# The second tile's edge masks made by two predicated copies on VectorE, and dense work divided among the attention blocks by another rule

## The chip, the core and the metric

The kernel runs on one core of a Trainium2 chip. A core has a matrix engine (TensorE, PE in the profile), a vector engine (VectorE, DVE), an engine for activation functions (ScalarE, ACT), GpSimd (POOL), and SyncE (SP), whose queue issues most of the DMAs here. The engines run side by side, each its own list of instructions in order, and wait for one another by semaphores. Data lies in HBM, in SBUF (128 partitions) and in PSUM (128 partitions, where TensorE writes its results).

The metric is the time of one execution on the device in microseconds (us); the median of several runs counts. The profiler traces one execution with the start and the length of its instructions, and its page and views sum these up.

## The reference

Four residual layers act on x (2048 rows, 640 columns), attention and feed-forward in turn, twice, all with the same weights.

```python
def _A_ref(x, wqkv, wo):
    H = 32; Dh = D // H; W = 256
    q, k, v = ...                        # (x @ wqkv), 32 heads of 20
    scores = jnp.einsum("bhqd,bhkd->bhqk", q, k) * (Dh ** -0.5)
    mask = (idx[:, None] - idx[None, :] >= 0) & (idx[:, None] - idx[None, :] < W)
    scores = jnp.where(mask[None, None], scores, -1e9)
    p = _softmax(scores, axis=-1)
    o = jnp.einsum("bhqk,bhkd->bhqd", p, v)
    return o.transpose(...).reshape(B, S, D) @ wo
def _B_ref(x, w1, b1, w2, b2):
    h = jnp.einsum("bsd,df->bsf", x, w1) + b1
    h = relu(h) ** 2
    return jnp.einsum("bsf,fd->bsd", h, w2) + b2
x = x + _A_ref(_layernorm(x), ...); x = x + _B_ref(_layernorm(x), ...)   # twice
```

A query sees the 256 keys up to and with its own. So of a block of scores of 64 keys by 64 queries, those on the two edges of this band are cut by a diagonal: on the near edge the keys behind the query's own position fall out, on the far edge those 256 or more before it.

## The kernel before

**Units and quads.** The 2048 rows are worked in units of T = 256 rows, 8 for each of the two pairs of layers, 16 in all (u = 0 to 15). A unit has dense work (projections to q, k and v, the projection after attention, the feed-forward layer) and attention work. Dense matmuls fill the whole 128x128 array; each product is a sum of three f16 matmuls (`mm3`, line 327). Attention works on quads of four heads, 8 quads a unit, n = 0 to 127. For units that have a unit of their own sequence before them (14 of 16, so 112 quads) the blocks are cut into tiles of 64 rows and a quad has three blocks on TensorE:

- M (`max_quad`, line 661): q times k with keys along the columns, only for each row's largest score. It works for a quad some places ahead (LEAD = 3). VectorE then moves the far-edge scores that count over others with a predicated copy (line 674, mask `maskq`) and reduces (line 677), for each of the two tiles e = 0 and 1.
- S (`exp_quad` and `halves_quad`, line 796): k times q with keys along the partitions, with the largest score subtracted by two more rows of the product. ScalarE takes the exponentials (line 781), two of 128x640 for each tile, into the SBUF tile `pt`. Then the band's edges are set to zero in `pt` by GpSimd's selects (line 809): for each tile, each of two edges (k) and each half of the partitions (h), one select on 64x256 elements, eight a quad. `masks[0]` holds the four jobs that the first two steps of V need, `masks[1]` those of the last two.
- V (`pv_quad`, line 874): probabilities times values, summed over four steps k; before step k it waits for `masks[k // 2]`. One part of its result goes to a bank that dense accumulators use too, and ScalarE copies it out (line 885); another goes to a spare part of M's and S's banks, and VectorE adds it (line 888, the job in `pvfree`).

S, M and V write the same six banks or wait for one another: S and M wait for the jobs in `bbjobs`, that is, M for the exponentials and S for the reductions.

Units 0 and 8 have whole tiles (lines 692, 830, 840); the change doesn't touch these but in a modelled time.

**The planner.** Each engine's order is written out when the program is built, by a model of time. `now` is TensorE's modelled clock. `post(eng, cost, fn, *deps, prio=...)` makes a job for an engine with a modelled cost; `pump` places jobs that can start, those of lower `prio` first, which `urgency` names by kind. `step(ns)` lets the clock go on by a dense piece of about 500 ns, and `Stream` hands out such pieces.

`together` (line 1162) lays the quads of one unit over dense work. `turns` gives two entries a quad, for S and for V; when an M is due it stands directly in front of V. Each entry has a part of the dense work, SHARE of a quad's between S and V and the rest between V and the next S. `work(part, w)` places dense pieces until that part is done and the jobs of the block are ready by the model. In front of V it is called again, with `pvfree`, the jobs of `masks[0]`, and those of `masks[1]` less 600 ns; where these aren't ready, dense pieces go between M and V.

`CARRY`, `KEEP` and `MID` are amounts of dense work kept for the last unit, for what follows its last quad, and for a place within it.

Of the kernel before, what the change touches and what calls it, by code (L numbers as in the profile page):

```python
# [16 lines left out]
P = 128  # L17
# [28 lines left out]
def kernel(ctx: ExitStack, tc: tile.TileContext, x, wqkv, wo, w1, b1, w2, b2, out):  # L46
# [11 lines left out]
    nc.vector.memset(neghalf, -0.5)  # L58
    masks = sb.tile([P, 3 * P], BF16, name="pt", tag="pt", bufs=2)
    maskq = sb.tile([P, Q], BF16, name="maskq")  # L60
    maskw = sb.tile([P, 2 * P], BF16, name="maskw")
# [9 lines left out]
    for h in range(2):  # L71
        nc.gpsimd.tensor_copy(maskq[h * Q:(h + 1) * Q, :], masks[h * Q:(h + 1) * Q, (h + 4) * Q:(h + 5) * Q])
    b1s = sb.tile([P, FC], F32, name="b1s")
    kts = []
# [30 lines left out]
    LOOK, LAT, LAND, CROSS, WLAND = 250.0, 50.0, 1800.0, 3600.0, 4500.0  # L105
    rate = [335.0]
    TAIL = {"A": 115.0, "D": 85.0, "G": 40.0, "S": 0.0}
# [66 lines left out]
    def step(ns):  # L174
        now[0] += ns
        pump()
# [142 lines left out]

    urgency = {"out": 0, "od": 0.5, "cross": 1, "mask": 0.5, "turn": 0.5, "exp": 0.5, "ln": 1, "y": 0.5}  # L320

# [303 lines left out]
    def max_quad(n, later=False):  # L625
# [19 lines left out]
        if quarters(u):  # L645
# [20 lines left out]
            by_tiles(pieces)  # L666
            now[0] += 763.0
            for e in range(2):
# [18 lines left out]
        else:  # L687
            for w in range(4):
                j, i = divmod(w, 2)
                for e in range(2):  # L690
                    r, p = slice(64 * e, 64 * e + 3 * DH), 2 * qd + j
                    nc.tensor.matmul(bb[e][:, w % 3, w // 3 * T:w // 3 * T + (1 + i) * P], qt[r, p, i * P:(i + 1) * P],  # L692
                                     cur[r, p, :(1 + i) * P], start=True, stop=True)
            now[0] += 440.0
            for w in range(4):
# [87 lines left out]
    def halves_quad(n, u, qd, qt, flat):  # L783

        pieces = []
        for j in range(2):
            for h in range(2):
                for kb, (o, q0, w) in PARTS[h].items():
                    kt, k0 = kts[(u if kb >= 2 else u - 1) % 3], kb % 2 * P + h * Q
                    a, b = (10 * j + o) * Q, (10 * j + o + w) * Q  # L790
                    cuts = [a] + [z for z in (512, 1024) if a < z < b] + [b]
                    for c0, c1 in zip(cuts, cuts[1:]):

                        def put(e, kt=kt, k0=k0, j=j, q=q0 * Q + c0 - a, c0=c0, c1=c1, h=h):
                            r = slice(64 * e, 64 * e + 3 * DH + 2)
                            nc.tensor.matmul(flat[e][h * Q:(h + 1) * Q, c0:c1], kt[r, 2 * qd + j, k0:k0 + Q],  # L796
                                             qt[r, 2 * qd + j, q:q + c1 - c0], start=True, stop=True,
                                             tile_position=(64 * e, 64 * h))

                        pieces.append((h, c1 - c0, put))  # L800
        by_tiles(pieces)
        now[0] += 763.0
        boxes, masks = [{}, {}], [[], []]
        for e, box in enumerate(boxes):

            def mask(k, h, box=box):
                r = slice(h * Q, (h + 1) * Q)
                m = box["pt"].rearrange("p (g c) -> p g c", g=4)[r, :, 4 * Q * k:4 * Q * k + Q]
                nc.gpsimd.affine_select(out=m, in_=m, pattern=[[0, 4], [-1 if k else 1, Q]], base=0, fill=0.0,  # L809
                                        compare_op=ALU.is_gt if k else ALU.is_ge, channel_multiplier=1 if k else -1)  # L810

            exps = []
            for j in range(2):
                exps.append(post("A", 584, power(box, flat[e], 10 * Q * j, 10 * Q * (j + 1)), *exps, prio=urgency["exp"]))
            bbjobs.extend(exps)
            for at, (k, h) in enumerate(((0, 0), (1, 1), (1, 0), (0, 1))):
                masks[at // 2].append(post("G", 415, lambda k=k, h=h, mask=mask: mask(k, h), *exps,
                                           prio=0 if n > NQ * NU - 4 else urgency["mask"]))
        return boxes, masks

    def whole_quad(n, u, qd, qt, flat):
# [3 lines left out]
        for k in range(2):  # L825
            w = T - k * P
            for j in range(2):
                for e in range(2):
                    r = slice(64 * e, 64 * e + 3 * DH + 2)
                    nc.tensor.matmul(flat[e][:, 512 * k + w * j:512 * k + w * (j + 1)], cur[r, 2 * qd + j, k * P:(k + 1) * P],  # L830
                                     qt[r, 2 * qd + j, k * P:T], start=True, stop=True)
        now[0] += 530.0
        for k in range(2):
# [16 lines left out]
    def pv_quad(n, quad):  # L850
# [8 lines left out]
        for k in range(4 if halves else 2):  # L859
            need(*masks[k // 2 if halves else k])  # L860
            for j in range(2):
                for e in range(2):
                    jj = 2 * j + e
                    c = (4 * qd + jj) * (DH + 1)
                    for h in range(2 if halves else 1):
# [5 lines left out]
                        else:  # L871
# [4 lines left out]
                                         skip_group_check=True, tile_position=(h * Q, 32 * jj))  # L876
            now[0] += (450.0, 230.0, 330.0, 285.0)[k] if halves else 400.0
        if qd == 0:
# [244 lines left out]

    SHARE = 0.5
    ALONE = 0.7
# [36 lines left out]
    def together(ns, ms, dense, cost, share=1.0, whole=True, after=None, pace=0):  # L1162
# [6 lines left out]

        def work(part, w):  # L1170

            nonlocal done
            while True:
                t = when(w) if w else None
                ready = t is not None and t <= now[0]
                if done >= cost * share * part / total and (ready or not w):
                    return
                c = s.go()
# [7 lines left out]
        for k, (part_, what, m) in enumerate(ts):  # L1186
# [6 lines left out]
            if kind == "s":  # L1193
                wants += pvfree
            work(part, Want(*wants, bank=False))
            if kind == "s":
# [27 lines left out]

    QKC, VC, OC, FCST, LNC, CARRY, KEEP, MID = 16.4e3, 8.2e3, 8.2e3, 39.2e3, 1.2e3, 22e3, 28e3, 10e3

# [77 lines left out]
    for u in range(1, NU):  # L1304
        last = u == NU - 1
        if u == 2:
            urgency.update({"out": 0, "od": 1, "cross": 0.5, "mask": 0, "turn": 0.5, "exp": 0.5, "ln": 0.5, "y": 1})
        quads, ahead = range(NQ * u, NQ * (u + 1)), range(NQ * u + LEAD, NQ * (u + 1) + LEAD)
# [46 lines left out]
```

## Time and profile before

| what | value |
|---|---|
| median of three runs | 1592.25 us (1591.53 to 1593.83) |
| the profiled execution, and its span | 1591.27 us, 1589.5 us |
| mean granted TensorE clock of the profiled execution | 0.997 of full speed |
| exponentials, line 781 | 512, 684 ns in the mean |
| selects, line 809 | 896, 440 ns in the mean, 394.0 us in all |
| predicated copies of line 674 | 224, 425 ns in the mean |
| reductions, line 677 | 224, 1222 ns in the mean |
| selects: shortest, median, longest | 406, 413, 1022 ns |

How to read the views. The page gives busy times by engine, the chain of work that ended last, and groups of instructions (line, engine, operation, output<-inputs, shapes, count; busy us, mean ns of one; the engine's idle time before them and what ended most of it). PE are matmuls, PEld the loads of their stationary operand. A row of the timeline has the start from the span's beginning, the length from the first instruction's start to the last one's end (us), engine, line, operation and a count where several were merged, and in brackets an idle time before it with what ended it. Matmuls overlap in their pipeline: what one costs is seen from start to start, not from its length. Where V's rows are shown, the first of its 64 stands for the block. A row of a line's own view, such as "POOL pt L809: 16.4, 64", names who ended the engine's idle time before that line's instructions, the sum in us, and how many times.

### The profile page before, as it was taken

How to read it: one execution, taken by the hardware profiler on the slowest of the kernel's cores; microseconds unless marked ns; L12 is line 12 of the kernel's file. 1: busy time of each engine (PE TensorE's matmuls, PEld its weight loads, DVE VectorE, ACT ScalarE, POOL GpSimd, SP SyncE). 2: the span in 40 equal slices, each digit the busy share in tenths (PEclk: the TensorE clock that was granted, in tenths of full speed). 3: DMA queues.
4: the chain of work that ended last, by engine and by line, in shares of the span. 5: the costliest groups of instructions: out<-in, count | busy, mean ns of one | idle time of the engine just before them, and what ended most of it. 6: DMA issues, size and time to landing. Idle time of an engine off the chain costs nothing.

```text
span 1589.5 us, 59412 instructions
## 1 busy us (share of the span) xinstructions
PE 1558.7 (98%) x25842; PEld 1200.2 (76%) x25842; DVE 971.3 (61%) x2022; ACT 669.1 (42%) x1369; POOL 636.2 (40%) x1291
## 2 busy tenths in 40 slices
PE   8989999999999999999999999999999999999989
PEld 7667777777777877778777777877778777786767
DVE  8787675655756466565565756566665656656432
ACT  4554435344343433434344343434434344443512
POOL 1224435344352533535233353533535344354612
PEclk9999999999999999999999999999999999999999
DMA  9874254442434334343352535425343351431020
GB/s 272 205 207 101 53 120 90 119 96 72 117 76 127 85 96 111 67 119 80 109 125 74 119 74 125 99 82 121 60 121 92 103 115 51 115 79 58 30 66 18
DMA packets 243375, 160.90 MB, mean 101 GB/s; under 512 B 91177, under 2 KB 226857, under 8 KB 243113
## 3 DMA queue, kind: packets, MB, share of 16 engines
q1 hardware_dynamic: 236744, 147.58, 38.2%
q10 hardware_dynamic: 6368, 9.50, 2.0%
q8 instruction: 203, 3.33, 0.9%
q14 instruction: 60, 0.48, 0.1%
HBM read 84.68 MB, written 52.95 MB: 87 GB/s over the span
## 4 chain that ended last, share of the span: by engine, by line
PE 92%; DVE 3%; DMA 1%; ACT 1%; issue 1%; POOL 1%; SPq 0%; POOLq 0%; ACTq 0%; DVEq 0%
PE acc L327 70%; PE pv L874 8%; PE bb L796 5%; PE bb L661 5%; PE bb L874 3%; DVE bb L641 1%; DVE mx L677 0%; ACT pt L781 0%; DMA kt<-in_B_w_dram 0%; PE spin L341 0%; PE bb L830 0%; PE bb L692 0%; POOL pt L809 0%; DMA o<-ot 0%; DMA qt<-mT 0%
## 5 line engine op out<-in xcount | busy, mean ns | idle before, releaser
L809 POOL TENSOR_SCALAR_AFFINE_SELECT pt<-pt 64x256 f32<-64x256 f32 x896 | 394.0, 440 | 523.4 <-ACT pt L781 458.0
L781 ACT ACTIVATE pt<-bb 128x640 f32<-128x640 f32 (+2 forms) x512 | 309.6, 684 | 245.9 <-PE bb L796 214.0
L327 PE MATMUL acc<-y,w_s 128*128 128x256 f16 x2880 | 336.3, 274 | 1.2 <-ACT y L377 0.6
L327 PE MATMUL acc<-w_s,hh 128*128 128x320 f16 (+1 forms) x2340 | 329.3, 297 | 0.0
L327 PEld LDWEIGHTS <-w_s 128*128 128x128 f16 x2880 | 275.8, 98 | 44.0 <-issue 2.4
L327 PEld LDWEIGHTS <-hh 128*128 128x128 f16 x2340 | 220.5, 98 | 87.2 <-issue 0.6
L677 DVE TENSOR_REDUCE mx<-bb 128x4 f32<-128x1024 f32 x224 | 273.8, 1222 | 6.3
L327 PE MATMUL acc<-yT,wq_s 128*128 128x256 f16 x2250 | 259.5, 273 | 2.2 <-DVE qd L510 0.7
L327 PEld LDWEIGHTS <-wq_s 128*128 128x128 f16 x2400 | 229.2, 98 | 37.4 <-issue 3.5
L674 DVE COPY_PREDICATED bb<-maskq,bb 128x256 f32<-128x256 uint16 x224 | 95.2, 425 | 156.0 <-PE bb L661 138.0
L1065 POOL TENSOR_TENSOR r<-r 128x256 f32<-128x256 f32 x192 | 120.3, 647 | 162.8 <-ACT r L1061 159.9
L1071 DVE TENSOR_TENSOR hh<-r,hh 128x256 f16<-128x256 f32 x192 | 94.7, 527 | 144.4 <-ACT hh L1068 135.9
L874 PE MATMUL pv<-pt,vt 64*32 64x128 f32 (+5 forms) x3840 | 180.7, 303 | 0.8 <-issue 0.6
L885 ACT COPY ot<-pv 128x256 f32<-128x256 f32 x128 | 47.5, 371 | 281.0 <-PE bb L874 260.8
L874 PE MATMUL bb<-pt,vt 64*32 64x192 f32 (+3 forms) x3584 | 164.2, 301 | 0.6 <-POOL pt L809 0.3
L874 PEld LDWEIGHTS pv<-pt,vt 64*32 64x32 f32 (+1 forms) x3840 | 128.4, 106 | 38.0 <-POOL pt L809 9.0
L327 PE MATMUL acc<-wo_s,od 128*128 128x320 f16 x960 | 142.8, 302 | 5.3 <-ACT od L965 2.8
L327 PE MATMUL acc<-wq_s,yT 128*128 128x320 f16 x900 | 132.8, 299 | 1.1 <-DVE y L378 0.5
L327 PEld LDWEIGHTS <-od 128*128 128x128 f16 x960 | 91.4, 98 | 46.9 <-ACT od L965 3.5
L874 PEld LDWEIGHTS bb<-pt,vt 64*32 64x32 f32 x3584 | 118.1, 105 | 10.7 <-POOL pt L809 7.1
L1061 ACT ACTIVATE r<-acc,b1s 128x256 f32<-128x256 f32 x192 | 80.7, 471 | 100.6 <-PE acc L327 98.3
L1068 ACT CAST hh<-r 128x256 f16<-128x256 f32 x192 | 74.5, 408 | 91.2 <-POOL r L1065 90.4
(99 smaller groups left out, 1376.1 us busy)
## 6 DMA issues: line engine op xcount, KB each, us to landing
qt<-qk SPq DMA_DIRECT2D x30, 480.0 KB
kt<-qk SPq DMA_DIRECT2D x30, 480.0 KB
qk<-qd SPq DMA_DIRECT2D x17, 640.0 KB
o<-ot SPq DMA_DIRECT2D x256, 42.0 KB
od<-o SPq DMA_DIRECT2D x14, 640.0 KB
qk<-yl SPq DMA_DIRECT2D x13, 640.0 KB
qk<-qd SPq DMA_DIRECT2D x17, 320.0 KB
xt<-in_A_x_dram SPq DMA_DIRECT2D x16, 320.0 KB
```

The source lines that it names most:

```text
L327: nc.tensor.matmul(acc, lhs(a, c), rhs(b, c), start=(k == 0), stop=(k == 3 * nk - 1))
L661: nc.tensor.matmul(flat[e][rows, o:o + b - a], qt[r, p, i * P + 64 * h:i * P + 64 * (h + 1)], kt[r, p, a + to:b + to], start=True, stop=Tr ...
L674: nc.vector.copy_predicated(wins[:, :, 4 * Q:], later, wins[:, :, :Q])
L677: nc.vector.tensor_reduce(most, wins[:, :, Q:], axis=mybir.AxisListType.X, op=ALU.max)
L781: return lambda: nc.scalar.activation(room_of(box)[:, a:b], bank[:, a:b], AF.Exp, scale=SCALE / (QS * QS))
L796: nc.tensor.matmul(flat[e][h * Q:(h + 1) * Q, c0:c1], kt[r, 2 * qd + j, k0:k0 + Q], qt[r, 2 * qd + j, q:q + c1 - c0], start=True, stop=Tru ...
L809: nc.gpsimd.affine_select(out=m, in_=m, pattern=[[0, 4], [-1 if k else 1, Q]], base=0, fill=0.0, compare_op=ALU.is_gt if k else ALU.is_ge, ...
L874: nc.tensor.matmul(pv[h][32 * jj:32 * (jj + 1), q0 * Q:(q0 + w) * Q], vf[r, c:c + 32], boxes[e]["pt"][r, a:b], start=(k == 0), stop=(k == ...
L1061: nc.scalar.activation(box["r"], acc[:, f, :], AF.Relu, bias=b1s[:, f0 + f:f0 + f + 1], scale=1.0 / (YS * WS))
L1065: nc.gpsimd.tensor_tensor(box["r"], box["r"], box["r"], op=ALU.mult)
L1068: nc.scalar.copy(hh[:, 0, f, :], box["r"])
L1071: nc.vector.tensor_sub(hh[:, 1, f, :], box["r"], hh[:, 0, f, :])
```

## The change

For the second tile (e = 1) of each of the 112 quads with half tiles, the four selects on GpSimd are replaced by two predicated copies on VectorE, one for each edge k, over all 128 partitions and 256 elements, that write zeros where a mask `drop` says so. Both stand in `masks[0]` and `masks[1]`. The first tile keeps its four selects. `drop` is made once at the start.

The planner is changed too: the modelled costs of S, M and V; 110 ns that the next dense piece is charged after each of these blocks; the order of urgencies, and from which unit on the second set of them holds; SHARE 0.6 instead of 0.5; CARRY 18 and MID 8 us instead of 22 and 10. In front of an M that is followed by V, `work` takes a further condition `hope`: beyond its part it goes on with dense pieces until `pvfree` and the masks are at most 600 ns (`masks[0]`) and 1200 ns (`masks[1]`) away, or 3 us of dense work have been done above the part.

```diff
+    edges = sb.tile([P, 2, P], BF16, name="pt", tag="pt", bufs=2)
+    drop = sb.tile([P, 2, Q], BF16, name="drop")
+    zero = sb.tile([P, 1], F32, name="zero")
+    nc.vector.memset(zero, 0.0)
+    nc.vector.memset(edges, 1.0)
...
+    nc.gpsimd.affine_select(out=edges[:, 0], in_=edges[:, 0], pattern=[[-1, P]], compare_op=ALU.is_gt,
+                            fill=0.0, base=0, channel_multiplier=1)
+    nc.gpsimd.affine_select(out=edges[:, 1], in_=edges[:, 1], pattern=[[1, P]], compare_op=ALU.is_ge,
+                            fill=0.0, base=0, channel_multiplier=-1)
+    for h in range(2):
+        nc.gpsimd.tensor_copy(drop[h * Q:(h + 1) * Q], edges[h * Q:(h + 1) * Q, :, h * Q:(h + 1) * Q])
...
-    rate = [335.0]
+    rate, apart, SWITCH = [335.0], [False], 110.0
...
     def step(ns):
-        now[0] += ns
+        now[0] += ns + (SWITCH if apart[0] else 0.0)
+        apart[0] = False
         pump()
...
-    urgency = {"out": 0, "od": 0.5, "cross": 1, "mask": 0.5, "turn": 0.5, "exp": 0.5, "ln": 1, "y": 0.5}
+    urgency = {"out": 0, "od": 0.5, "cross": 2, "mask": 0, "turn": 1, "exp": 0.5, "ln": 1, "y": 1, "clear": 0.5}
...
-            now[0] += 763.0
+            now[0] += 690.0
+            apart[0] = True
...
+            def clear(k, box=box):
+                m = box["pt"].rearrange("p (g c) -> p g c", g=4)[:, :, 4 * Q * k:4 * Q * k + Q]
+                nc.vector.copy_predicated(m, drop[:, k:k + 1, :].bitcast(mybir.dt.uint16).to_broadcast([P, 4, Q]),
+                                          zero.unsqueeze(1).to_broadcast([P, 4, Q]))
+
+            if e:
+                for k in range(2):
+                    j = post("D", 340, lambda k=k, clear=clear: clear(k), *exps, prio=urgency["clear"])
+                    masks[0].append(j)
+                    masks[1].append(j)
+                continue
...
-            now[0] += (450.0, 230.0, 330.0, 285.0)[k] if halves else 400.0
+            now[0] += (440.0, 225.0, 330.0, 305.0)[k] if halves else 420.0
+        apart[0] = True
...
-    SHARE = 0.5
+    SHARE = 0.6
+    HOPE = 3000.0
...
-                if done >= cost * share * part / total and (ready or not w):
-                    return
+                ahead = done - cost * share * part / total
+                if ahead >= 0 and (ready or not w):
+                    t = when(hope) if hope and ahead < HOPE else 0.0
+                    if t is not None and t <= now[0]:
+                        return
...
-            work(part, Want(*wants, bank=False))
+            hope = None
+            if kind == "v" and m is not None:
+                hope = Want(*pvfree, bank=False, soon=[(j, 600.0) for j in quad[1][0]] + [(j, 1200.0) for j in quad[1][-1]])
+            work(part, Want(*wants, bank=False), hope)
...
-    QKC, VC, OC, FCST, LNC, CARRY, KEEP, MID = 16.4e3, 8.2e3, 8.2e3, 39.2e3, 1.2e3, 22e3, 28e3, 10e3
+    QKC, VC, OC, FCST, LNC, CARRY, KEEP, MID = 16.4e3, 8.2e3, 8.2e3, 39.2e3, 1.2e3, 18e3, 28e3, 8e3
...
-        if u == 2:
-            urgency.update({"out": 0, "od": 1, "cross": 0.5, "mask": 0, "turn": 0.5, "exp": 0.5, "ln": 0.5, "y": 1})
+        if u == 1:
+            urgency.update({"out": 0, "od": 1, "cross": 0.5, "mask": 0, "turn": 0.7, "exp": 0.5, "ln": 0.5, "y": 0.5, "clear": 0})
```

More of the change, by code (lines that the diff above doesn't have):

```diff
@@ L693, in max_quad @@
                                      cur[r, p, :(1 + i) * P], start=True, stop=True)
-            now[0] += 440.0
+            now[0] += 530.0
+            apart[0] = True
             for w in range(4):
@@ L801, in halves_quad @@
         by_tiles(pieces)
-        now[0] += 763.0
+        now[0] += 690.0
+        apart[0] = True
         boxes, masks = [{}, {}], [[], []]
@@ L831, in whole_quad @@
                                      qt[r, 2 * qd + j, k * P:T], start=True, stop=True)
-        now[0] += 530.0
+        now[0] += 540.0
+        apart[0] = True
         for k in range(2):
@@ L876, in pv_quad @@
                                          skip_group_check=True, tile_position=(h * Q, 32 * jj))
-            now[0] += (450.0, 230.0, 330.0, 285.0)[k] if halves else 400.0
+            now[0] += (440.0, 225.0, 330.0, 305.0)[k] if halves else 420.0
+        apart[0] = True
         if qd == 0:
@@ L1168, in together, with work @@
         s = Stream(dense)
-        def work(part, w):
+        def work(part, w, hope=None):
             nonlocal done
```

## The prediction

> **What bounds the kernel now.** I read the page's first and fourth parts, the waits, a table by windows, and then the timeline around single quads. The page first: span, busy time by engine, and the chain that ended last.
>
> ```profile
> span 1589.5 us, 59412 instructions
> PE 1558.7 (98%) x25842; PEld 1200.2 (76%) x25842; DVE 971.3 (61%) x2022; ACT 669.1 (42%) x1369; POOL 636.2 (40%) x1291
> PE 92%; DVE 3%; DMA 1%; ACT 1%; issue 1%; POOL 1%; SPq 0%; POOLq 0%; ACTq 0%; DVEq 0%
> ```
>
> TensorE is busy 98% of the span and makes 92% of the chain; no other engine is near full. So time can only come off in two ways: TensorE waits less, or its own instructions take less. The change alters no matmul. The profiled execution took 1591.27 us, 1.77 us more than its span and 0.98 us under the median of 1592.25 us; a saving worked out on it is taken off the median unchanged.
>
> The next fence has one unit of the steady middle by windows (columns: window, length, busy us of PE, PEld, DVE, ACT, POOL), and from the view of line 874, whose matmuls multiply probabilities and values, the row that says for what TensorE stood idle in front of it.
>
> ```profile
> 850.00:946.30 96.30, 96.29 (x1601) 74.44 (x1600) 59.03 (x111) 39.90 (x82) 38.15 (x79) 1.00 0.40 98
> ...
>   POOL pt L809: 16.4, 64
> ```
>
> A unit of eight quads takes 96.30 us, 12.04 us a quad. TensorE waited 64 times, 16.4 us in all, for the masks that GpSimd makes with the selects of line 809. That is the largest wait the change can touch.
>
> Now the order inside a quad, by starts on TensorE. L796 is the score block (S), L661 the block for the maxima of a later quad (M), L874 the values block (V, first row shown), L327 dense work.
>
> ```profile
> 869.93 5.09 PE L327 MATMUL acc<-yT,wq_s 128*128 128x256 f16 x45
> 874.95 0.76 PE L661 MATMUL bb<-kt,qt 60*64 60x256 f16 x38
> 875.64 0.40 PE L874 MATMUL pv<-pt,vt 64*32 64x256 f32 x1
> 876.94 1.27 PE L327 MATMUL acc<-yT,wq_s 128*128 128x256 f16 x10
> ...
> 1309.80 0.76 PE L661 MATMUL bb<-kt,qt 60*64 60x256 f16 x38
> 1310.49 0.72 PE L327 MATMUL acc<-y,w_s 128*128 128x256 f16 x5
> 1311.14 0.40 PE L874 MATMUL pv<-pt,vt 64*32 64x256 f32 x1
> 1312.44 4.12 PE L327 MATMUL acc<-y,w_s 128*128 128x256 f16 x35
> ```
>
> Start to next start: 45 dense matmuls take 5.02 us, 5 take 0.65. So one costs (5.02 - 0.65) / 40 = 0.109 us, and each run of dense work costs 0.65 - 5 x 0.109 = **0.10 us on top**, whatever its length. M takes 0.69 whether V or dense follows, V takes 1.30 whether M or dense stood before it. So a short dense run between M and V costs 0.10 us more than the same matmuls put into the next run. Such runs stand between M and V in 47 of the 112 quads with half-tile masks; of the short ones (up to ten matmuls) these are the first and the last.
>
> ```profile
> 291.03 0.72 PE L327 MATMUL acc<-w_s,hh 128*128 128x320 f16 x4
> ...
> 1485.22 0.72 PE L327 MATMUL acc<-y,w_s 128*128 128x256 f16 x5
> ```
>
> **The change part by part.**
>
> *The masks.* One quad with its neighbours on all engines:
>
> ```profile
> 886.82 0.76 PE L661 MATMUL bb<-kt,qt 60*64 60x256 f16 x38
> 887.62 0.43 DVE L674 COPY_PREDICATED bb<-maskq,bb 128x256 f32<-128x256 uint16 x1
> 888.09 1.22 DVE L677 TENSOR_REDUCE mx<-bb 128x4 f32<-128x1024 f32 x1
> 888.88 4.83 PE L327 MATMUL acc<-wo_s,od 128*128 128x320 f16 x33
> 889.90 0.42 DVE L674 COPY_PREDICATED bb<-maskq,bb 128x256 f32<-128x256 uint16 x1
> 890.43 0.42 DVE L888 TENSOR_TENSOR ot<-bb,ot 128x256 f32<-128x256 f32 x1
> 890.77 1.21 DVE L677 TENSOR_REDUCE mx<-bb 128x4 f32<-128x1024 f32 x1
> 893.64 0.76 PE L796 MATMUL bb<-qt,kt 62*64 62x128 f16 x38
> 894.58 2.49 ACT L781 ACTIVATE pt<-bb 128x640 f32<-128x640 f32 x4 [5.16 <-PE bb L796]
> 895.95 4.30 POOL L809 TENSOR_SCALAR_AFFINE_SELECT pt<-pt 64x256 f32<-64x256 f32 x8 [1.65 <-ACT pt L781]
> 898.65 0.76 PE L661 MATMUL bb<-kt,qt 60*64 60x256 f16 x38
> 899.34 0.40 PE L874 MATMUL pv<-pt,vt 64*32 64x256 f32 x1
> 900.89 2.36 PE L327 MATMUL acc<-yT,wq_s 128*128 128x256 f16 x20
> ```
>
> From S's start the four exponentials end at +3.43 us, the eight selects at +6.61. V starts at +5.70 and takes 1.55 instead of 1.30: its last part waits for the last selects. After the change GpSimd has four selects, 4 x 0.54 (4.30 / 8) from +2.31, done at +4.5; VectorE starts two copies behind the last exponential. The trace has no predicated copy on this tile. Nearest row: line 674 with the same 128x256 elements, 0.43; its operands lie elsewhere (scores in PSUM). Bounds for one copy: 0.42, a lone 128x256 operation on SBUF, and 0.56, the same one beside GpSimd, both shown below under the rivals; I take 0.43. Two end at +4.4 (+4.7 at the upper bound, if VectorE is free). So the masks are ready about 2 us sooner.
>
> *Where V will stand.* The share of dense work between S and V rises from 0.5 to 0.6. Dense time of a quad: 12.04 - 0.69 (S) - 0.69 (M) - 1.30 (V) - 0.21 (two runs) = 9.15 us. V comes at 0.69 + 0.10 + 0.6 x 9.15 + 0.69 = +6.97 us, 2.3 us after the later mask. The 16.4 us can go between not at all and wholly; I take **11 us**, two thirds, since the waits in the first unit, in the last two (less dense work a quad) and in three quads without an M have less cover. Once they go, V follows M at once; what is late next is the bank into which the next dense run writes, and that wait stays.
>
> *Fewer runs.* Dense work now goes on in front of M until the masks are nearly there, by up to 3 us more than the share asks, instead of splitting in two around M. Bounds: none of the 47 runs goes, or all, 4.9 us. I take 42, **4.4 us**, for with masks at +4.7 M and V fit together in nearly every quad. The Trainium skill (TensorEngine Tiling, Key Properties) says that a change of tiling mode drains TensorE, not only a change between dense and tiled; M and V here use different tile shapes, so by it M next to V would still pay one of the two drains and the saving be 2.2 us, the sum 1583. The trace disagrees: M is 0.69 and V 1.30 with or without dense work between.
>
> *VectorE's bill.* 224 copies x 0.43 = 96 us more, 971 to 1067 us, 67% of the span. In the chain VectorE holds 3%, 48 us, of which I let a tenth more come back in proportion to the tenth more work: **4 us** lost (bounds: nothing, and 0.10 us a quad or more, the fourth rival). Queued behind a copy that waits for its exponential stand evictions of dense accumulators, the reductions of line 677 and the sum of line 888; the next dense run waits for the first, S for the others. The cover is that exponentials end 3.5 us before V, and S, M and V stand apart.
>
> *GpSimd's relief.* 448 selects x 0.44 go, 197 us. GpSimd is off the path but for V's wait, so this is worth nothing beyond the masks.
>
> *The rest.* The planner's constants (cost of S, M, V, 110 ns for a switch, urgencies, 4 us of dense work moved out of the last unit) change order only: 0, with 2 us either way. Setup adds two selects, two small copies and two memsets. Nearest rows:
>
> ```profile
> L63 DVE MEMSET maskw<- 128x128 uint32 x1 | 0.2, 165 | 0.0
> masks.py:199 POOL TENSOR_SCALAR_AFFINE_SELECT ident<-ident 128x128 f32<-128x128 f32 x1 | 0.3, 294 | 0.1
> L72 POOL COPY maskq<-pt 64x64 bf16<-64x64 bf16 x2 | 0.5, 232 | 0.1
> ```
>
> Some 0.2 us on VectorE and 2 x 0.294 + 2 x 0.232 = 1.05 us on GpSimd, once, at the start; I count nothing for it. No DMA is added or moved past a queue.
>
> **Sum:** -11 - 4.4 + 4 = -11.4 us. 1591.27 becomes 1579.9; on the median's scale 1592.25 - 11.4 = **1581 us**.
>
> **The rivals.**
>
> *1. Copies and selects hold each other up.* Line 1071's subtraction has two inputs in SBUF, as the new copy has (mask and zero):
>
> ```profile
> 1133.73 1.47 POOL L1065 TENSOR_TENSOR r<-r 128x256 f32<-128x256 f32 x2 [1.54 <-ACT r L1061]
> 1134.92 0.56 DVE L1071 TENSOR_TENSOR hh<-r,hh 128x256 f16<-128x256 f32 x1 [0.19 <-ACT hh L1068]
> 1135.67 0.43 DVE L1071 TENSOR_TENSOR hh<-r,hh 128x256 f16<-128x256 f32 x1 [0.19 <-ACT hh L1068]
> ...
> L1071 DVE TENSOR_TENSOR hh<-r,hh 128x256 f16<-128x256 f32 x192 | 94.7, 527 | 144.4 <-ACT hh L1068 135.9
> ```
>
> With GpSimd at work it took 0.56 us, with GpSimd idle 0.43; the mean of all is 527 ns. The second tile's copies run just when the first tile's selects run. The cost would be 224 x 0.13 = 29 us of VectorE; V has 2.3 us of cover, so it decides only where that is used up. If half of the wait for masks stays (5.5) and VectorE's bill grows by 1.4: 1588 us. The Trainium skill (SBUF — State Buffer, Who interferes with whom) states such a lock for VectorE with two SBUF inputs against a GpSimd operation that reads SBUF; these rows agree.
>
> *2. The order doesn't change.* If the new condition in front of M seldom binds, the short runs stay: 1581 + 4.4 = 1585 us. For it: 65 of 112 quads already go without. Against: the masks come 2 us sooner.
>
> *3. The wait moves from selects to copies.* If VectorE reaches the copies late, V waits as long for them: only 4.4 - 4 is left, 1592 us, no change. It needs copies that start 2.5 us after the last exponential, two reductions of 1.22 us in front. At 61% busy that is rare.
>
> *4. Slower: S waits for the reductions.* With 0.4 x 9.15 = 3.66 us of dense work between V and S instead of 4.76 (888.88 to 893.64), S comes 1.0 us earlier after V. The second reduction ended at 891.98, 1.66 us before S; 0.66 us is left. If displaced evictions make it 1.0 us late, S waits 0.34 us; in half of the quads, 56 x 0.34 = 19 us: 1600 us. It decides from 11.4 / 112 = 0.10 us a quad, a reduction 0.76 us late. Against it: the planner lays dense work in front of S when it sees the reduction late, so only what it misjudges (2 x 0.13 us of copies) counts.
>
> **How the numbers follow.** Forecast 0.55; first rival 0.12 (1588); second 0.13 (1585); third 0.10 (1592); fourth 0.10 (1600). About 0.2%, 3.2 us, is what a measurement here can tell from no change, so faster means under 1589.1. The forecast, the second and most of the first lie there: **0.79**; the third and the first's rest within: **0.11**; slower **0.10**. The low end is all of 16.4 and 4.9 with nothing lost, 1571; the high end reaches the third rival, 1592; the fourth and the far tails are left out.
>
> **What would show it.** Right: the wait of line 874 for GpSimd's masks falls from 16.4 to a few us; under ten dense runs between M and V; a unit of about 95.6 us instead of 96.30; VectorE near 1067 us, GpSimd near 440. Wrong: line 874 waiting for the new copies (third), the copies well over 0.5 us with waits for masks left (first), the short runs still there (second), or TensorE idle in front of line 796 for VectorE (fourth).

## The result and the profile after

| | median us | lowest to highest | executions |
|---|---|---|---|
| before | 1591.89 | 1591.45 to 1593.83 | 4 |
| after | 1573.45 | 1572.40 to 1574.43 | 4 |

The ratio is 0.9882 (95% interval 0.9865 to 0.9899): 18.4 us less, where 11.4 were forecast. The profiled execution took 1573.51 us, 17.8 less than that of before, with a span of 1571.8. From the page of the changed kernel: span, busy time by engine, the chain by engine, and of the groups the first tile's selects and the new copies.

```profile
span 1571.8 us, 58938 instructions
...
PE 1541.4 (98%) x25842; PEld 1202.1 (76%) x25842; DVE 1041.4 (66%) x2248; ACT 669.1 (43%) x1369; POOL 453.6 (29%) x847
...
PE 79%; DVE 7%; POOL 2%; issue 2%; ACT 1%; DMA 0%; SPq 0%; ACTq 0%; DVEq 0%; POOLq 0%
...
L824 POOL TENSOR_SCALAR_AFFINE_SELECT pt<-pt 64x256 f32<-64x256 f32 x448 | 195.4, 436 | 619.2 <-ACT pt L795 589.7
...
L833 DVE COPY_PREDICATED_SCALAR pt<-drop,zero 128x256 f32 x224 | 99.7, 498 | 178.9 <-ACT pt L795 178.2
```

In the changed file the score block S is line 810, M 673, V 901, dense work 339, the selects 824, the copies 833, the reductions 690, the exponentials 795. The view of V's line says for what TensorE stood idle in front of it.

```profile
its engine sat idle before it (us, times) until:
  issue: 3.7, 18
  POOL pt L867: 2.2, 8
  POOL r L1093: 0.2, 1
  DVE bmv L369: 0.2, 1
  DVE pt L833: 0.2, 1
```

The selects, 16.4 us and 64 times before, are gone from the list (line 867 belongs to the units with whole tiles); the copies took their place once, for 0.2 us. One quad by the timeline of the changed kernel, with one row for V:

```profile
869.49 0.76 PE L810 MATMUL bb<-qt,kt 62*64 62x128 f16 x38
870.18 5.63 PE L339 MATMUL acc<-yT,wq_s 128*128 128x256 f16 x50
870.34 2.49 ACT L795 ACTIVATE pt<-bb 128x640 f32<-128x640 f32 x4 [3.69 <-PE bb L810]
871.76 1.84 POOL L824 TENSOR_SCALAR_AFFINE_SELECT pt<-pt 64x256 f32<-64x256 f32 x4 [9.73 <-ACT pt L795]
872.94 0.89 DVE L833 COPY_PREDICATED_SCALAR pt<-drop,zero 128x256 f32 x2 [2.86 <-ACT pt L795]
...
875.74 0.76 PE L673 MATMUL bb<-kt,qt 60*64 60x256 f16 x38
876.43 0.40 PE L901 MATMUL pv<-pt,vt 64*32 64x256 f32 x1
...
877.73 2.90 PE L339 MATMUL acc<-yT,wq_s 128*128 128x256 f16 x25
```

From S's start the last exponential ends at +3.34 us, the selects at +4.11, the copies at +4.34. V starts at +6.94 and takes 1.30 (876.43 to 877.73), with nothing between M and V. That is the forecast order and nearly its times: copies at +4.4, V at +6.97; the selects, forecast at +4.5, are done 0.4 sooner.

**Where the 17.7 us of span came from.** I divided both traces at the first V row of the 17th quad (unit 2) and of the 113th (unit 14): a start, a middle of twelve units, and the end with what follows the last quad. By windows (length, busy us of PE, PEld, DVE, ACT, POOL, then TensorE's granted clock), the kernel before:

```profile
0.00:206.40 206.40, 191.56 (x2715) 144.26 (x2715) 153.58 (x390) 103.29 (x206) 68.36 (x141) 0.99 0.63 168
206.40:1358.30 1151.90, 1148.60 (x19703) 889.96 (x19699) 701.58 (x1410) 481.99 (x984) 479.13 (x976) 1.00 0.41 98
1358.30:1586.40 228.10, 218.51 (x3429) 165.96 (x3428) 115.85 (x222) 83.78 (x179) 88.75 (x175) 0.99 0.22 58
```

and the changed kernel, with one unit of its middle:

```profile
0.00:215.40 215.40, 195.47 (x2725) 146.79 (x2726) 161.24 (x410) 103.21 (x206) 51.55 (x109) 0.96 0.58 160
215.40:1352.80 1137.40, 1134.45 (x19700) 890.20 (x19696) 754.96 (x1584) 480.28 (x984) 338.75 (x624) 1.00 0.41 99
1352.80:1568.80 216.00, 211.45 (x3432) 165.09 (x3428) 124.89 (x253) 85.60 (x179) 63.31 (x114) 0.99 0.22 61
...
850.00:945.30 95.30, 95.23 (x1599) 74.33 (x1597) 63.09 (x125) 39.74 (x82) 28.91 (x53) 1.00 0.40 99
```

The stretches hold the same matmuls, to within ten. The start is 9.0 us longer, the middle 14.5 shorter (1.2 a unit), the end 12.1 shorter. Only the middle was in my sum. To see what they are made of, I took each block's time on TensorE from its start to the next block's start, less its bare cost from the prediction (S and M 0.69, V 1.30, a dense run 0.10 and 0.109 a matmul of 256 columns, others in proportion to their columns); S, M and V here are those of the 112 quads with half tiles. In the middle V's excess falls from 9.4 us to 0.2, the dense runs from 226 to 192 (34 x 0.10 = 3.4) and their excess from 3.9 to 0.9; S's excess rises from 4.0 to 5.2. With five dense matmuls fewer (0.5) and the blocks with whole tiles 0.6 longer that makes the 14.5. The end's 12.1 are V (3.0), S (2.6), the excess of dense runs (3.3), seven runs fewer (0.7) and the transposes of line 391 (3.4), with M 0.9 longer. Over the whole execution V's excess goes from 18.4 to 5.3, dense runs from 312 to 266, and runs between M and V from 47 to 2.

Of the 5.3, 4.2 stand at one place, behind the first V of unit 1. It is the dense run after this V that waits there, not V for a mask, and the kernel before has 3.7 us at the same place:

```profile
126.36 7.04 PE L339 MATMUL acc<-wo_s,od 128*128 128x320 f16 x30 [3.81 <-ACT od L993]
```

### The profile page after: what moved, and what is told of

Read it like the earlier page. It is cut to its first block, busy times and chain, and to the rows that moved or that the text cites. A ratio compares the mean times of both kernels' runs of the same rounds, so it can differ in the third digit from the quotient of the medians.

```text
span 1571.8 us, 58938 instructions
## 1 busy us (share of the span) xinstructions
PE 1541.4 (98%) x25842; PEld 1202.1 (76%) x25842; DVE 1041.4 (66%) x2248; ACT 669.1 (43%) x1369; POOL 453.6 (29%) x847
## 4 chain that ended last, share of the span: by engine, by line
PE 79%; DVE 7%; POOL 2%; issue 2%; ACT 1%; DMA 0%; SPq 0%; ACTq 0%; DVEq 0%; POOLq 0%
PE acc L339 61%; PE pv L901 6%; PE bb L810 5%; PE bb L673 4%; DVE mx L690 2%; PE bb L901 2%; POOL bmv L376 1%; POOL pt L824 1%; ACT pt L795 1%; DVE xt L378 1%; DVE bb L687 1%; DVE x L1128 0%; DVE bst L365 0%; DVE ot L916 0%; DVE bb L653 0%
## 5 line engine op out<-in xcount | busy, mean ns | idle before, releaser
L824 POOL TENSOR_SCALAR_AFFINE_SELECT pt<-pt 64x256 f32<-64x256 f32 x448 | 195.4, 436 | 619.2 <-ACT pt L795 589.7
L339 PE MATMUL acc<-y,w_s 128*128 128x256 f16 x2880 | 328.9, 273 | 1.3 <-DVE y L390 1.2
L833 DVE COPY_PREDICATED_SCALAR pt<-drop,zero 128x256 f32 x224 | 99.7, 498 | 178.9 <-ACT pt L795 178.2
L901 PE MATMUL pv<-pt,vt 64*32 64x192 f32 (+5 forms) x3840 | 167.8, 304 | 0.5 <-POOL pt L867 0.3
L901 PE MATMUL bb<-pt,vt 64*32 64x64 f32 (+3 forms) x3584 | 153.9, 301 | 0.0
```

The lines of the kernel that those rows point to most:

```text
L339: nc.tensor.matmul(acc, lhs(a, c), rhs(b, c), start=(k == 0), stop=(k == 3 * nk - 1))
L833: nc.vector.copy_predicated(m, drop[:, k:k + 1, :].bitcast(mybir.dt.uint16).to_broadcast([P, 4, Q]), zero.unsqueeze(1).to_broadcast([P, 4, ...
L901: nc.tensor.matmul(pv[h][32 * jj:32 * (jj + 1), q0 * Q:(q0 + w) * Q], vf[r, c:c + 32], boxes[e]["pt"][r, a:b], start=(k == 0), stop=(k == ...
```

## The experiments

Theory A: the gain is the sooner masks, and the planner's constants fit the new timing. Rival B: it is the planner's order, which the masks merely permit. Rival C: the copies cost VectorE much more than is seen, and something else pays for it. The same three stretches tell the runs apart; the stretches are bounded as above in each trace, and "runs" are dense runs in the middle.

| kernel | median us (before beside it) | ratio, 95% | start | middle | end | runs |
|---|---|---|---|---|---|---|
| before, profile above | 1591.89 | | 206.4 | 1151.9 | 228.1 | 226 |
| before, once more | 1591.27 (one execution) | | 207.5 | 1152.3 | 226.6 | 226 |
| after, profile above | 1573.45 (1591.89) | 0.9882, 0.9865 to 0.9899 | 215.4 | 1137.4 | 216.0 | 192 |
| after, once more | 1575.51 (1591.70) | 0.9900, 0.9886 to 0.9914 | 218.7 | 1137.3 | 216.8 | 192 |
| masks only | 1576.74 (1592.27) | 0.9901, 0.9886 to 0.9917 | 215.8 | 1142.2 | 225.7 | 193 |
| masks only, once more | 1580.11 (1591.70; one execution) | | 209.0 | 1140.0 | 226.3 | 193 |
| planner only | 1621.44 (1592.27) | 1.0189, 1.0168 to 1.0210 | 220.5 | 1163.3 | 234.0 | 192 |
| no `hope` | 1587.12 (1592.27) | 0.9964, 0.9950 to 0.9978 | 215.2 | 1138.8 | 231.5 | 192 |
| copies twice | 1602.93 (1592.27) | 1.0069, 1.0050 to 1.0088 | 216.4 | 1154.1 | 224.3 | 192 |
| unit 1 with selects | 1578.19 (1589.85) | 0.9918, 0.9902 to 0.9933 | 219.9 | 1139.0 | 216.0 | 192 |
| CARRY 22, MID 10 | 1582.46 (1589.85) | 0.9955, 0.9942 to 0.9967 | 216.9 | 1137.5 | 223.3 | 193 |
| zero as a whole tile | 1581.91 (1589.85) | 0.9949, 0.9934 to 0.9963 | 217.5 | 1141.9 | 218.2 | 192 |
| SHARE 0.5 | 1588.44 (1589.85) | 0.9989, 0.9979 to 0.9998 | 215.8 | 1142.3 | 225.6 | 205 |
| "turn" 0.45 | 1583.03 (1591.70) | 0.9947, 0.9933 to 0.9961 | 218.5 | 1134.9 | 224.6 | 192 |

The stretches are those of the one profiled execution, the median is that of several. The profiled one of "masks only" took 1588.42 us, 11.7 more than its median; its repetition is the better guide.

**Masks only.** The kernel before with the copies in place of the second tile's selects, and none of the planner's changes (the copies get an urgency of their own).

```diff
+            if e:
+                for k in range(2):
+                    j = post("D", 340, lambda k=k, clear=clear: clear(k), *exps, prio=urgency["clear"])
...
```

> The kernel before with the copies alone: no other planner constant, share 0.5, no further condition in front of M. Theory A (sooner masks carry the gain): masks are ready about 4.5 us after S and V stands at about 5.7, so the waits of V for masks (16.4 us) go to under 3 us and most of the 47 short runs between M and V go too; 1592 falls to 1575-1580. Theory B (the planner's new order carries it): waits for masks fall somewhat but the runs stay at over 35; 1585-1590.

15.5 us less: within the intervals, all of the gain. In the middle V's excess is 2.6 us instead of 9.4 (by the repetition, as all that follows), and dense runs fall to 193 with nothing changed in the planner: masks that are ready sooner let M and V stand together by themselves. In V's view the selects (now line 820) are down from 16.4 us and 64 times to

```profile
  POOL pt L820: 1.3, 4
  DVE pt L829: 0.5, 2
```

The end stays at 226. There, and once in the start, S (line 807) now waits for VectorE's reductions, as the fourth rival said, where the kernel before has one such wait of 0.2 us:

```profile
  DVE mx L688: 4.7, 3
```

Both profiles of this kernel have these three waits. All that TensorE waits for VectorE, by its waits view, is 21.9 us here, 14.6 before and 11.6 in the changed kernel. So with the old planner the copies do have a price, and it is with the whole change that it isn't seen.

> The copies alone with the planner of before, for a second profile: the profiled execution of the first run took 1588.4 us, 12 us more than the median of 1576.7. Expected 1575-1579; if the gain of 16 us lies in the middle and not in the last two units, the middle twelve units take about 1138-1142 us instead of 1151.9 and the end still 225.

This one execution took 1580.11 us, 3.4 above the median of the first six: enough to say where the time lies, not to rank it against the whole change.

**Planner only.** The changed kernel with four selects for the second tile too.

```diff
-            if e:
-                for k in range(2):
-                    j = post("D", 340, lambda k=k, clear=clear: clear(k), *exps, prio=urgency["clear"])
...
-                continue
```

> The changed kernel with the second tile's masks again by four selects on GpSimd; all planner constants, share 0.6 and the condition in front of M stay. Theory A: the selects end about 6.6 us after S, where V would now stand at 7.0, but the planner's own time for them holds M back or leaves runs, and waits of 5 us or more stay; 1582-1589. Theory B: V stands late enough anyway, waits and runs both go; 1573-1578, and the copies were not needed.

29 us slower than before, beyond both ranges that were expected. The view of its V line (879) and TensorE's waits:

```profile
  POOL pt L813: 16.4, 57
```

```profile
PE acc L328 <- ACT ot L891: 8.8, 12, 1.8
```

The runs have gone here too (192), but V now stands directly behind M with no dense work between, and still waits 16.4 us for the selects; the dense run behind V then waits for the copy out of the bank that V shares with it. In the middle V's excess is 14.8 us and that of dense runs 11.7. Only 11 us of the loss lie in the middle; the start is 14 longer than before, the end 6. B falls: the order alone loses, and only with the copies is it harmless.

**No `hope`.** The changed kernel without the new condition in front of M.

```diff
-    HOPE = 3000.0
+    HOPE = 0.0
```

> The changed kernel without the further condition in front of M (its limit set to zero). If the condition is what joins V to M, 30 or more short runs come back, 0.10 us each: 1577-1579. If sooner masks and the share of 0.6 are enough, under ten come back and the time stays at 1573-1575.

The middle has 192 runs and 1138.8 us as with it. The condition isn't what joins M to V. The time is 10 to 13 us longer all the same, by the ratios, which neither expectation had, and the profile has it in the end: 231.5 instead of 216.0 us (its execution took 1590.28 us, 3.2 more than the median).

**Copies twice.** Each copy of the second tile is made twice, over the same elements.

```diff
-                for k in range(2):
+                for k in (0, 1, 0, 1):
```

> The changed kernel with every one of the 224 copies made twice (the second writes the same zeros), 112 us more work for VectorE, all of it told to the planner. It measures the price of a copy on the path. Prediction's term: 4 us for the first 224; as VectorE fills, the second 224 should cost at least that, 1578 or more. Theory C (VectorE has room, the price is nothing): under 2 us, 1572-1575.5.

27 to 30 us more than the changed kernel, by the ratios (1.0069 less 0.9900 or 0.9882, of 1592). The page, TensorE's waits, and one unit by windows:

```profile
PE 1544.5 (97%) x25842; PEld 1202.6 (75%) x25842; DVE 1131.5 (71%) x2472; ACT 671.1 (42%) x1369; POOL 439.2 (27%) x847
```

```profile
PE acc L339 <- DVE yl L522: 8.1, 12, 0.7
...
PE bb L810 <- DVE ot L916: 3.1, 6, 1.1
```

```profile
850.00:946.00 96.00, 95.20 (x1529) 74.13 (x1527) 65.74 (x127) 39.65 (x85) 28.21 (x54) 1.00 0.41 98
```

VectorE goes from 66 to 71%. What waits is dense work for its accumulators to be moved out: the dense runs' excess in the middle goes from 0.9 to 12.1 us, S's from 5.2 to 8.5. One case by the timeline:

```profile
334.12 1.66 DVE L833 COPY_PREDICATED_SCALAR pt<-drop,zero 128x256 f32 x4 [0.34 <-ACT pt L795]
...
342.73 1.01 DVE L522 SCALAR_TENSOR_TENSOR yl<-acc,yl 128x512 f16<-128x512 f32 x2
...
343.46 1.25 PE L339 MATMUL acc<-wq_s,yT 128*128 128x320 f16 x8 [0.72 <-DVE yl L522]
```

So C is right for the second 224 copies, which cost some 28 us. For the first it is right with the old planner, by the waits under "Masks only", and isn't seen in the whole change. The planner knows of the additional copies and orders the rest anew, so this is the price of the work with its order, not of the queue alone.

**Zero as a whole tile.** The copied value has 128x64 elements in SBUF instead of one a partition, so that the copy reads two tensors from there.

```diff
-    zero = sb.tile([P, 1], F32, name="zero")
+    zero = sb.tile([P, Q], F32, name="zero")
```

> The changed kernel with the zeros read from a tile of 64 columns in SBUF, broadcast, instead of one column: the same result, but the copy then has two whole inputs in SBUF. First rival's mechanism: copies beside GpSimd's selects get longer (0.56 us instead of 0.50 or 0.43) and the selects too, toward 0.54 us from 0.44; with V's cover of about 2 us this gives 0 to 3 us, 1573-1577; if half of V's wait for masks comes back, 1579 or more. If copies keep one length with and without GpSimd, there is no such lock for this operation.

8 to 11 us more than the changed kernel, by the ratios. From the groups of this kernel:

```profile
L824 POOL TENSOR_SCALAR_AFFINE_SELECT pt<-pt 64x256 f32<-64x256 f32 x448 | 205.7, 459 | 615.5 <-ACT pt L795 576.5 <-PE acc L339 17.1
L833 DVE COPY_PREDICATED pt<-drop,zero 128x256 f32<-128x256 uint16 x224 | 120.1, 587 | 173.5 <-ACT pt L795 172.7 <-POOL pt L824 0.2
```

The copies' line has in its own view (count, then shortest, median and longest ns), here

```profile
L833 DVE COPY_PREDICATED pt<-drop,zero x224: 432/644/860, 121.8 to 1508.3; 128x256 f32<-128x256 uint16 x112
```

and in the changed kernel

```profile
L833 DVE COPY_PREDICATED_SCALAR pt<-drop,zero x224: 480/499/514, 120.3 to 1499.6; 128x256 f32 x112
```

With one value a partition the instruction is another form (the name has SCALAR), and takes 480 to 514 ns whether GpSimd works or not. With a tile it takes 587 in the mean, a select 459 instead of 436. Ten of its copies ran while GpSimd was idle, by the trace, and took 432 to 452 ns; beside GpSimd one took up to 860. So the lock of the first rival is real, and the change's form of the copy avoids it. By the Trainium skill (SBUF — State Buffer, Who interferes with whom) a VectorE instruction with at most one SBUF input, outside its 2-port modes, doesn't contend with GpSimd, and one with two contends with a GpSimd instruction that reads SBUF. Both runs agree: 480 to 514 ns in the one form, up to 860 beside GpSimd in the other. The price doesn't fall on V, whose excess in the middle stays 0.2 us, but on S, 5.2 to 10.1. Its line's view in this kernel has

```profile
  DVE ot L916: 5.2, 15
```

15 waits for VectorE's sum, where the changed kernel has one of 1.0 us.

**Unit 1 with selects, CARRY 22 and MID 10, SHARE 0.5.** The copies left out of the first unit that has them, and two settings put back, to find what makes the start longer and the end shorter.

```diff
-            if e:
+            if e and u > 1:
```

> The changed kernel, but in unit 1, while VectorE still converts weights, the second tile's masks are made by four selects on GpSimd as before. In the two profiles the stretch up to unit 2's first V grew from 206.4 to 215.4 us. Theory D (the copies there are the bill that the prediction put at 4 us): about 9 us come back, 1563-1567. Rival (the loss there is the planner's new urgencies and order, or chance of that profile; the run with the planner alone, without copies, lost 14 there): 1571-1576.

```diff
-    QKC, VC, OC, FCST, LNC, CARRY, KEEP, MID = 16.4e3, 8.2e3, 8.2e3, 39.2e3, 1.2e3, 18e3, 28e3, 8e3
+    QKC, VC, OC, FCST, LNC, CARRY, KEEP, MID = 16.4e3, 8.2e3, 8.2e3, 39.2e3, 1.2e3, 22e3, 28e3, 10e3
```

> The changed kernel with the amounts of dense work kept for the last unit as before (22 and 10 us instead of 18 and 8). The last two units and what follows them went from 228.1 to 216.0 us in the profiles. If the moved dense work brings most of these 12 us: 1579-1586. If they come from the masks and from the condition in front of M (without it the same stretch took 231.6): 1571-1576.

```diff
-    SHARE = 0.6
+    SHARE = 0.5
```

> The changed kernel with the share of dense work between S and V back at 0.5. Fourth rival's place: in the changed kernel S waits 0.3 us once a unit for VectorE's sum of line 916; with S about 0.9 us later that should go, 12 x 0.3 = 3.6 us less in the middle, while V, about 0.9 us earlier, still finds its masks ready (at about 4.6 us after S, V at 6). So 1568-1573 if the new share only costs; 1576 or more if the share is what keeps V from waiting.

Without copies in unit 1 the start is 219.9 us: taking them out doesn't give the 9 us back, and the time, 1578.19 us, is above both ranges that were expected. With the old CARRY and MID the end is 223.3 instead of 216.0, with the old SHARE 225.6. TensorE's waits in the end of the kernel before begin with

```profile
PE bb L391 <- DVE xt L366: 3.3, 1, 3.3
```

It is one wait of the transposes of line 391 for a layer norm's output `xt` from VectorE. The ends of masks only, planner only, no `hope` and of these two settings have the same wait of 3.3 us; the changed kernel has none in either profile. With SHARE 0.5 thirteen runs come back in the middle, 1142.3 us, while S's excess there falls from 5.2 to 2.8.

**"turn" 0.45.** S's wait for VectorE was left, about once a unit. By the timeline of the changed kernel:

```profile
290.10 0.82 DVE L456 TENSOR_TENSOR yl<-xt,yl 128x640 f16<-128x640 f32 x1
290.84 1.22 DVE L690 TENSOR_REDUCE mx<-bb 128x4 f32<-128x1024 f32 x1
...
292.39 0.48 DVE L1128 SCALAR_TENSOR_TENSOR x<-acc,x 128x320 f32<-128x320 f32 x1
292.79 0.41 DVE L916 TENSOR_TENSOR ot<-bb,ot 128x256 f32<-128x256 f32 x1
292.95 1.06 PE L810 MATMUL bb<-qt,kt 62*64 62x128 f16 x38
293.95 4.52 PE L339 MATMUL acc<-w_s,hh 128*128 128x320 f16 x32
```

The low half of a normalised block (line 456), 0.82 us, stands in front of the second reduction, so VectorE's sum is late and S takes 1.00 from start to start instead of 0.69. The edit lets the jobs named "turn" (reductions among them) go first.

```diff
-            urgency.update({"out": 0, "od": 1, "cross": 0.5, "mask": 0, "turn": 0.7, "exp": 0.5, "ln": 0.5, "y": 0.5, "clear": 0})
+            urgency.update({"out": 0, "od": 1, "cross": 0.5, "mask": 0, "turn": 0.45, "exp": 0.5, "ln": 0.5, "y": 0.5, "clear": 0})
```

> The changed kernel with the urgency of the reductions at 0.45 instead of 0.7 from unit 1 on, so that VectorE does them and the sum of line 916 ahead of layer norm's and the splits' work. S's wait of 0.3 us once a unit should go, 3 us and more: 1568-1572. Rival: what is pushed back (splits, layer norms) is late for the dense work in turn, 1576 or more.

The middle is 1134.9 us, 2.5 less (hardly beyond what two profiles of one kernel differ by, see below), and S's excess there 2.9; but the end is 8 to 9 us longer, where S now waits for the reductions. TensorE's waits from 1353 us to the end:

```profile
PE bb L810 <- DVE mx L690: 5.9, 5, 1.8
```

No version beat the changed kernel. The setting only for the middle units wasn't tried.

**The kernels of before and after, once more.** On one chip, to see by how much two profiles of a kernel differ.

> The kernel before, unchanged, for a second profile. In its first profile the stretch up to unit 2's first V took 206.4 us; in every profile since, with copies, planner changes or both, 215 to 220. If the change costs the start 9 us, this one shows 205-208 again; if that first profile's start was lucky, 213-218.

> The changed kernel, unchanged, as the control for the runs of this study on the same chip: 1571-1576, and middle stretches of 95.3 us a unit with waits of V for masks of nearly nothing.

The middles agree within 0.4 us and the ends within 1.5, the starts within 1.1 and 3.3. The two profiles of masks only lie further apart, 2.2 us in the middle and 6.8 in the start. So differences of 2 to 3 us in the middle and of less than 7 in the start mean little. The 9 us at the start are beyond that: before 206.4 and 207.5, after, its variants and planner only 215.2 to 220.5.

## Why the prediction was right, and where not

**V's wait for the masks, -11: right in size and place.** V's excess fell by 13.1 us in the whole execution; the wait for selects has no row left in V's view. The 16.4 us of that row were idle time in front of V's line, nearly all of it before the weight loads (9.0 and 7.1 on the page of before), so the start-to-start times are the better measure. What is left is not, as the prediction had it, waits in the first unit and the last two that have less cover: 4.2 of the 5.3 us are the dense run's wait shown above.

**Fewer dense runs, -4.4: right in size, wrong in cause.** 46 runs went, 46 x 0.10 = 4.6 us, and with the masks alone as many (265 left). The step said that this comes from dense work going on in front of M "until the masks are nearly there". Without that condition the middle has as many runs, and with the copies alone 193: sooner masks are enough, for V's needs are then met as soon as M is. V and M side by side still cost 1.30 and 0.69, so the whole 0.10 us of a run is saved and not half of it. Whether the 0.69 holds a drain, whatever follows M, no run here shows; the prediction's "The trace disagrees" says more than the trace does.

**The copy, 0.43 us: too low for one, right for two.** One takes 0.50, within the bounds of 0.42 and 0.56 (the lone row shown for the lower bound has 0.43), but a pair takes 0.87 to 0.90, for the second starts before the first has ended; 2 x 0.43 was the sum's figure. From 3.43 that makes +4.29; the prediction's +4.4 has 0.1 more that it doesn't name, and the pair did start 0.11 us behind the last exponential.

**VectorE's bill, +4: mis-sized, and by a wrong working.** In the whole change no such loss is seen: S's excess goes from 8.3 us to 6.3 (6.9 and 8.0 in the second profiles), up 1.2 in the middle with waits of the kind that the fourth rival named, once a unit and not in every second quad; the excess of dense runs falls by 1.8. With the copies alone it is seen: S's excess is 11.8, and TensorE's waits for VectorE are 7 us more. The working took a tenth of the 3% that VectorE held in the chain. That share is no price: in the changed kernel it is 7%, and the time is less. The second set of copies met the bound of "0.10 us a quad or more", 28 / 112 = 0.25 us a quad, and its first victim was dense work that waits for its accumulators.

**The rest, 0 with 2 us either way: near as a net, wrong in its parts.** I took the planner's constants for mere order. Against the masks alone the whole change is 0 to 3 us faster, by the ratios. But that is about 10 us in the end (226 to 216) and 3 in the middle (1140.0 to 1137.4), against a start that is longer: 215.4 and 218.7, with the masks alone 209.0 and 215.8. By the sum: V and the runs took 13.1 + 4.6 = 17.7 us off the span, where 15.4 were forecast. All else, forecast at +4, came to nothing: beyond V and the runs the start is 10.2 longer, the middle 1.9 and the end 8.4 shorter. That these cancel is luck, for the working has none of the three. In the end the settings work together: each of HOPE, CARRY with MID, SHARE and "turn" put elsewhere loses 7 to 16 us there, though in the middle they matter by 5 us at most. The 3.3 us wait of the transposes is the part of it that the traces name for HOPE, CARRY and SHARE; the rest is spread over V, S and dense runs.

What makes the start longer is known in part. Planner only has 220.5 us without a copy, so the constants are enough for it. Of the 9 us, 5.1 are idle time of TensorE (14.8 before, 19.9 after, length less busy). Dense runs wait there for accumulators to be moved out: 2.9 us until VectorE has made `qd` (0.7 before) and 1.9 until ScalarE has made `ot` (none before). Planner only has these two as well, 2.8 and 2.2 us; masks only has neither at that length. The rest is longer matmuls at a granted clock of 0.96 instead of 0.99. The clock isn't fixed by the program: the two profiles of masks only have 0.96 with a start of 215.8 us, and 0.98 with 209.0. Whether a lower clock follows the idle time or the other way, these runs don't tell, and of the urgencies in question only "turn" was tried singly.

**The rivals.** The first (lock) didn't occur in this kernel, whose copy has only one whole SBUF tensor as input, but does as soon as it has two. The second (order doesn't change) is refuted by the 2 runs between M and V that are left of 47. The third (wait moves to the copies) by one wait of 0.2 us. The fourth (S waits for the reductions) came with the copies alone, three waits of 4.7 us together; in the whole change S loses only some 0.3 us about once a unit to VectorE's sum.

**The signs named in advance.** A unit of about 95.6 us: 95.30. VectorE near 1067, GpSimd near 440: 1041 and 454. VectorE is lower although the copies add 99.7 us. In part others became shorter (see below); in part an operation that starts before the last has ended counts once, as with the pair of copies.

## What to carry to other kernels

If a matrix block waits for its masks, move a part of them to an engine that is idle at that moment, and judge the taker by what waits on it next, not by its mean filling. VectorE is 66% full with the copies under either planner; under the old one TensorE waits 7 us more for it than before, under the new one 2 to 3 less. A second set of copies, at 71%, cost some 28 us. Choose the form of the operation that reads one SBUF tensor when GpSimd works beside it. Constants that only set an order are not free where the program starts and ends; look at those stretches on their own, before and after.

## What was not expected of the hardware

A predicated copy with one value a partition is a form of its own, slower alone than that with a tensor (480 to 514 ns against 432 to 452 for 128x256) and faster beside GpSimd (498 against 587 in the mean of all).

One of VectorE's operations on two SBUF tensors became shorter. From the groups by line, before and after:

```profile
L968 DVE TENSOR_TENSOR od<-od 128x320 f16<-128x320 f32 x56 | 33.1, 610 | 8.3 <-ACT od L965 7.5
```

```profile
L996 DVE TENSOR_TENSOR od<-od 128x320 f16<-128x320 f32 x56 | 29.5, 545 | 2.0 <-ACT od L993 1.2
```

With the copies alone it takes 530 ns in the mean (repetition), with the planner alone and all selects 569. So under either planner it is shorter with half of the selects, and the order has a share of its own.

A kernel with one order of instructions varied more than expected: twelve executions of the one without `hope` lay between 1580.99 and 1591.85 us (granted clock 0.989 to 0.994), while seventeen of the kernel before on the same chip lay between 1588.56 and 1594.92 (0.995 to 0.998).
